# Sliding-window attention and a spectral mix on one core: q and k loaded as one block of long rows and transposed on 64x64 array tiles; the imaginary weight of mode 0 loaded again

## The chip, the cores and the metric

The kernel runs on one core of a Trainium2 chip. The time is the device time of one execution in microseconds (us). Of the kernel before, three runs are at hand: 453.2, 453.93 and 454.9 us, so the median is 453.93 us. The profiled execution took 453.2 us. Lower is better.

## The reference, cut to what matters

Two stages follow each other. The first is attention with 8 batches, 8 heads, 576 tokens and 64 values per head, in a causal window of 128 tokens with a slope per head. The second works on its output, `x` of 8 x 576 x 512:

```
scores = q @ k.T / 8 - slope[h] * |i - j|         where 0 <= i - j < 128, else -1e9
x      = softmax(scores) @ v                      heads side by side: 8 x 576 x 512
X      = rfft(x over the tokens)[:64 modes]
Y[m]   = (Xr + i Xi)[m] @ (w_r + i w_i)[m]        64 complex 512 x 512 weights
u      = x + irfft(Y)
out    = u + relu(u @ w_ch)
```

The inputs are float32. `q`, `k` and `v` are 9.4 MB each, the 128 matrices of `w_r` and `w_i` are 1 MB each. Mode 0 of a real signal has no imaginary part, and the inverse transform takes no notice of an imaginary part of `Y[0]`; so `w_i[0]` cannot change the output.

## The kernel before, in words

**Attention.** A unit is half a batch: four heads of one `b`, so there are 16 units. `load` (L198) has SyncE (SP) issue the transfers of a unit: one for q, one for k (L220) and three for v (L208, L213), into raw float32 buffers of which there are two each. `cast` (L226) lets VectorE (DVE) turn them into bfloat16, and issues the load of the unit two further on into the buffer that is thereby free. `transpose` (L243) has TensorE (PE) turn the cast q or k into `tp` in PSUM, and `evacuate` (L254) brings `tp` into `qkT` in SBUF, with the tokens in order; ScalarE (ACT) does this, except for q of the first two units, which are DVE's. `score` (L262) multiplies k by q on 64x64 array tiles, two heads on the two row halves of the array; for two of its four tiles it first adds a bias with the identity (L272). `exp` (ACT), `mask` (DVE, L306), `value` (PE, L332) and `norm` (DVE, L347 and L348) end the unit; `spectrum` (PE, L369) and `channels` (ACT, L387 and L388) take the batch's transform after every second unit, into the table `XC`.

The order of the work is written by hand: `STAGE` (L38) lists which step of which unit comes next, and each engine works its instructions off in that order. In one stage the transposition of k comes after `channels` and ahead of the next `score` with bias; that of q comes behind a `value` and ahead of a `score` without bias. `tp` has one buffer in PSUM, which `spectrum` uses too, so that the transposition of k waits for `channels` in each second unit.

How q and k lie: a head is 576 tokens of 256 bytes. In the kernel before, a partition holds 9 tokens each of two heads, which lie apart in memory: two rows of 2304 bytes. Partitions 0 to 63 hold heads 0 and 2, partitions 64 to 127 hold heads 1 and 3. The cast puts the two heads side by side, so that 9 transpositions of 128 x 128 (one for each token place `j`) make `tp`: head dimension of heads 0 and 1 in the upper half of the partitions and of heads 2 and 3 in the lower.

**The spectral mix.** `load_w` (L440) loads one weight of 1 MB. During attention GpSimd (POOL) issues 14 such loads that cast to bfloat16 on the way, held back by a small copy (`gate`, L520) that waits for a given `norm`; at the end of attention 6 more go into the raw buffers of q, k and v (L449). Then SP issues the rest as float32 (L453) into 6 and later 2 more buffers, and 8 more casting loads go into the first buffers to come free (`again`). For each weight PE makes four matmuls (L650) into `acc`; after each fourth mode the result is scaled (L543) and transposed (L547). From group 7 on, other work is put between the weights: the projection with `w_ch` of the first half of the modes (L623, L587, L609). Mode 0's imaginary weight, number 1 of 128, is in no list: `todo_w` (L438) leaves it out, and the loop passes over it (L645), so 127 weights are loaded. Once the last weight is multiplied, a last stage (L707 to L792) finishes and stores the output.

Of the kernel before, what the change touches and what calls it, by code (L numbers as in the profile page):

```python
# [10 lines left out]
FP32 = mybir.dt.float32  # L11
BF16 = mybir.dt.bfloat16
# [8 lines left out]
P = 128  # L21
D = 64
# [5 lines left out]
FULL = 4  # L28
TAIL = 64

TPP = 9

W = D + 2

# [72 lines left out]
class _Attention:  # L107
# [90 lines left out]
    def load(self, w, u):  # L198
        nc = self.nc
        if u >= len(self.units):  # L200
            return
        b, g = self.units[u]
        hs = slice(4 * g, 4 * g + 4)
        if w == "v":
            t = self.raw[w][:, u % 2]
            sv = self.v[b, hs]
            for pair in range(2):
                nc.sync.dma_start(  # L208
                    out=t[:, pair],
                    in_=sv[:, 2 * pair * P : 2 * (pair + 1) * P].rearrange(  # L210
                        "h (p j) d -> p h (j d)", j=2),
                )
            nc.sync.dma_start(  # L213
                out=t[64:96, 2],
                in_=sv[:, FULL * P :].rearrange("h (p j) d -> p h (j d)", j=2),
            )
        else:
            t = self.raw[w][:, u % 2]
            src = (self.q, self.k)["qk".index(w)][b, hs]
            nc.sync.dma_start(  # L220
                out=t.rearrange("p e j d -> p e (j d)"),
                in_=src.rearrange("(e h) (p j) d -> (h p) e (j d)", h=2, j=TPP),
            )
        self.loaded[w, u] = t

    def cast(self, u, w):  # L226

        nc = self.nc
        src = self.loaded.pop((w, u))
        if w == "v":  # L230
            src = src.rearrange("p s h (j d) -> p s h j d", j=2)
            for half in range(2):
                row = slice(64 * half, 64 * half + 64)
                nc.vector.tensor_copy(  # L234
                    self.vb[u % 2][row, :, :, :, W * half : W * half + D], src[row, :2])
            nc.vector.tensor_copy(self.vt[u % 2][64:96, :, :, :D], src[64:96, 2])
        else:
            dst = self.mid.tile([P, TPP, 2, D], BF16, tag=w, name=w)
            nc.vector.tensor_copy(dst.rearrange("p j e d -> p e j d"), src)  # L239
            self.casted[u, w] = dst  # L240
        self.load(w, u + 2)

    def transpose(self, u, w):  # L243
        nc = self.nc
        src = self.casted.pop((u, w))
        if (u, w) == (0, "k"):
            tp = self.ps.tile([P, TPP, P], BF16, tag="sc", bufs=2, name="tp")
        else:
            tp = self.ps.tile([P, TPP, P], BF16, tag="tp", name="tp")
        for j in range(TPP):  # L250
            nc.tensor.transpose(tp[:, j], src[:, j].rearrange("p e d -> p (e d)"), self.ident)  # L251
        self.open[w, u] = tp

    def evacuate(self, u, w):  # L254
        tp = self.open.pop((w, u))
        dst = self.qkT[u % 2][:, "qk".index(w), :, : self.S]
        (self.nc.vector.tensor_copy if u < 2 and w == "q" else self.nc.scalar.copy)(  # L257
            dst.rearrange("q h (p j) -> q h p j", j=TPP),
            tp.rearrange("q j (h p) -> q h p j", h=2),
# [138 lines left out]
def kernel(  # L398
# [10 lines left out]
    nc = tc.nc  # L409
    ctx.enter_context(tc.manual_schedule(engines=ALL | {SP}))  # L410
    B, H, S, _ = q.shape
    NM, DM, _ = moe_w_r.shape
    AHEAD = {0: 1, 1: 1, 2: 1, 4: 1, 5: 1, 7: 1, 8: 1, 10: 1, 11: 1, 12: 1, 13: 3, 14: 1}
    LATER = {14: 3, 15: 3}
    EARLY, NWA, NWB, AGAIN = 14, 6, 2, 8
# [12 lines left out]
    early = actx1.enter_context(  # L428
        tc.tile_pool(name="w1", bufs=EARLY, side="right", reuse_waits="tile")
    )  # L430
    rawpool = actx1.enter_context(tc.tile_pool(name="raw", bufs=1, side="right"))
    raw = {w: rawpool.tile([P, 2, 2, TPP, D], FP32, name=w + "r") for w in "qk"}
    raw["v"] = rawpool.tile([P, 2, 3, 4, 2 * D], FP32, name="vr")
    spare = [raw[w][:, i].rearrange("p e j d -> p (e j d)") for w in "qk" for i in range(2)]
    vflat = raw["v"].rearrange("p u s h d -> p (u s h d)")
    spare += [vflat[:, 2 * DM * i :] for i in range(3)]
    spare = [t[:, : 2 * DM].bitcast(BF16).rearrange("p (a e) -> p a e", a=4) for t in spare]
    wq, homes, todo_w, again = {}, {}, [0, *range(2, 2 * NM)], []  # L438

    def load_w(n, pool, bf16, chosen=None):  # L440


        for i in ([i for i in todo_w if i not in again][:n] if chosen is None else chosen):
            todo_w.remove(i)
            src = (moe_w_r, moe_w_i)[i % 2][i // 2].rearrange("(p a) e -> p a e", a=4)
            homes[i] = pool
            if bf16:
                t = spare.pop(0) if pool is None else pool.tile([P, 4, DM], BF16, tag="w", name="w")
                nc.gpsimd.dma_start(out=t, in_=src)  # L449
                wq[i] = [t[:, a] for a in range(4)]  # L450
            else:
                t = pool.tile([P, 4, DM], FP32, tag="w", name="w")
                nc.sync.dma_start(out=t, in_=src)  # L453
                wq[i] = [t[:, a].bitcast(BF16)[:, 1::2] for a in range(4)]

    with ExitStack() as actx:
# [43 lines left out]
        for h in (0, 2):  # L500
# [4 lines left out]
        side = {0: [(at.offset, 4), (at.offset, 6), (at.decay, 5), (at.offset, 5), (at.decay, 7),  # L505
                    (at.offset, 7), (at.decay, 4), (at.decay, 6)]}
        lags = [lag for _, _, lag in STAGE]
        for stage in range(min(lags), n + max(lags)):
            for name, arg, lag in STAGE:
                run(name, arg, stage - lag)  # L510
                if name in ("transpose", "exp") and side.get(stage):
                    for _ in range(1 + (name == "transpose")):
                        fn, h = side[stage].pop(0)
# [11 lines left out]
    with ExitStack() as mctx:  # L525
# [6 lines left out]
        again = [first + 4 + 2 * i for i in range(AGAIN)]  # L532
# [100 lines left out]
        def warm():  # L633
            wt = ps.tile([P, DM], FP32, tag="warm", bufs=1, name="warm")
            for _ in range(6):
                nc.tensor.matmul(wt, lhsT=ident, rhs=wch[:, 0], start=True, stop=True)  # L636

        quads, side, recycle = [], [], list(again)
        ZW = Z = XW = wch = w2 = None
        K1 = again[-1] + 1  # L640
        for g in range(NM // 4):
            acc = ps.tile([P, DM], FP32, tag="acc", bufs=2, name="acc")
            for i in range(8):
                m, ri = 4 * g + i // 2, i % 2
                if 2 * m + ri not in wq:  # L645
                    continue
                w = wq[2 * m + ri]
                for a in range(4):
                    c0 = (a * NC + (8 if ri == 0 else 0)) * NM + m
                    nc.tensor.matmul(  # L650
                        acc[32 * (i // 2) : 32 * (i // 2) + 32],
                        lhsT=XC[:, c0 : c0 + 31 * NM + 1 : NM],
                        rhs=w[a],
                        start=(ri == 0 and a == 0), stop=(ri == (m > 0) and a == 3),
                        tile_position=(0, 32 * (i // 2)),
                    )
                k = 8 * g + i
                if recycle:
                    load_w(1, early, True, [recycle.pop(0)])
                elif homes[k] not in (early, None):  # L660
                    load_w(1, homes[k], False)
                if k == K1 - 1:
                    actx1.close()
                    w2 = mctx.enter_context(
                        tc.tile_pool(name="w2", bufs=NWB, side="right", reuse_waits="tile")
                    )
                    load_w(NWB, w2, False)
                    right = mctx.enter_context(
                        tc.tile_pool(name="late", bufs=1, side="right", reuse_waits="tile")
                    )  # L670
                    wch = right.tile([P, 4, DM], BF16, name="wch")
                    nc.gpsimd.dma_start(out=wch, in_=moe_w_ch.rearrange("(a p) e -> p a e", p=P))
                    ZW = right.tile([P, B // 2, 2, DM], BF16, name="ZW")
                    Z = right.tile([P, B, DM], BF16, name="Z")
                    XW = right.tile([P, len(units), 2, DM], BF16, name="XW")

                if quads:
                    if next(quads[0], True):
                        quads.pop(0)
                elif side and k % 5:  # L680
                    side.pop(0)()
                elif 8 * g + i >= 2 * NM - 5:
                    if 8 * g + i < 2 * NM - 1:
                        warm()
            end = quad_end(acc, g)
            next(end)
            quads.append(end)
            if g == 7:
                side += [partial(early_spectra, bp) for bp in range(B // 2)]
                side += [partial(project, j, n) for j in range(len(units)) for n in range(2)]  # L690
# [132 lines left out]
```

## Time and profile before

| what | value |
|---|---|
| median of three runs | 453.93 us (453.2 to 454.9) |
| the profiled execution's own time | 453.2 us |
| its span, first to last instruction | 451.4 us |
| mean granted TensorE clock | 0.901 |
| PE busy | 351.5 us (78%), 3288 matmuls |
| DVE busy | 173.3 us (38%) |
| ACT busy | 154.6 us (34%) |
| read from HBM, written to it | 162.53 MB, 9.44 MB |
| attention | 0 to about 131 us |
| weights | PE's first matmul of a weight starts at 130.9 us, the last at 408.6 us |
| last stage | to 451.4 us |

How to read the lines of a profile: a group line names the line of the kernel, the engine, the operation, what it writes and reads, the shape and the count; behind the first bar stand the busy time in us and the mean of one in ns, behind the second the idle time of the engine just ahead of such instructions and what ended it. In a view by stretches of time, each engine's busy us stands with the number of instructions in brackets, then the granted clock, the mean busy share of the 16 DMA engines (over 1 where packets of one engine overlap) and the GB/s that they wrote. In the chain of waits and in the timeline the first number is the start in us, the second the length. A busy PE is not PE at its peak: matmuls are pipelined, and the next one starts long before the one ahead has ended.

### The profile page before, as it was taken

To read this page: it belongs to the slowest core of one execution; us is meant where nothing else is said; L and a number is where in the kernel's file an instruction comes from. 1 tells how busy PE (TensorE), PEld (TensorE's weight loads), DVE (VectorE), ACT (ScalarE), POOL (GpSimd) and SP (SyncE) were. 2 spreads that over 40 slices of the span, in tenths; PEclk is the share of its full clock that TensorE was granted. 3 is DMA by queue.
4 is the path that set the end of the run, shared out by engine and by line. 5 is a ranking of instruction groups with operands and counts; after the bars stand their busy time and mean duration, and the time that the engine had idled before them with its cause. 6 is when DMAs were issued, how large, how long until landed. Compare 5 with 4: busy or idle time off the path is not lost.

```text
span 451.4 us, 7816 instructions
## 1 busy us (share of the span) xinstructions
PE 351.5 (78%) x3288; PEld 186.2 (41%) x3288; DVE 173.3 (38%) x314; ACT 154.6 (34%) x191; POOL 54.6 (12%) x86
## 2 busy tenths in 40 slices
PE   4788999999876644456576679998989898987892
PEld 3466777777653212112121233443333343333230
DVE  7889899998732101001010241211111121103684
ACT  6868999999800000000000011221111121104671
POOL 8610101002411100000000000000000000000562
PEclk9999999999989655567666999999999899999998
DMA  8999999999999999999999999999999999990598
GB/s 285 325 333 310 310 305 309 316 284 249 212 303 316 315 318 315 340 395 422 420 422 418 424 421 418 420 422 419 422 421 420 417 422 421 419 399 8 212 345 282
DMA packets 51730, 157.26 MB, mean 348 GB/s; under 512 B 3696, under 2 KB 22640, under 8 KB 39024
## 3 DMA queue, kind: packets, MB, share of 16 engines
q1 hardware_dynamic: 47136, 141.57, 81.6%
q0 software_dynamic: 4560, 15.21, 17.0%
q8 instruction: 25, 0.41, 0.4%
q14 instruction: 9, 0.07, 0.0%
HBM read 162.53 MB, written 9.44 MB: 381 GB/s over the span
## 4 chain that ended last, share of the span: by engine, by line
DMA 54%; PE 24%; DVE 13%; ACT 4%; issue 3%; POOL 1%; ACTq 0%; SPq 0%; DVEq 0%; POOLq 0%
DMA w<-in_moe_w_i_dram 42%; PE acc L650 7%; DMA vr<-in_moe_w_i_dram 6%; DMA w<-in_moe_w_r_dram 4%; PE av L332 3%; PE my L623 2%; DVE vb L234 2%; DVE x L348 2%; DMA qr<-in_q_dram 2%; DVE att L306 2%; DVE q L239 2%; PE tp L251 2%; PE yy L754 1%; PE xt L369 1%; PE warm L636 1%
## 5 line engine op out<-in xcount | busy, mean ns | idle before, releaser
L650 PE MATMUL acc<-w,XC 128*32 128x512 bf16 x484 | 134.0, 465 | 59.8 <-DMA w<-in_moe_w_i_dram 38.6
L650 PEld LDWEIGHTS <-XC 128*32 128x32 bf16 x508 | 57.1, 141 | 126.6 <-issue 101.7
L295 ACT ACTIVATE att<-sc 128x1024 bf16<-128x1024 f32 x64 | 64.0, 1031 | 7.5 <-PE sc L285 7.5
L629 ACT CAST XW<-my 128x512 bf16<-128x512 f32 x36 | 21.1, 586 | 109.0 <-PE my L587 109.0
L735 POOL TENSOR_TENSOR r<-r,x 128x1024 f32<-128x1024 f32 x8 | 17.1, 2131 | 271.6 <-ACT r L733 271.5
L543 DVE TENSOR_SCALAR yq<-acc 128x512 bf16<-128x512 f32 x14 | 9.7, 690 | 100.9 <-PE acc L650 100.9
L571 ACT CAST ZW<-zw 128x512 bf16<-128x512 f32 x4 | 2.3, 586 | 133.5 <-PE zw L566 133.5
L611 DVE COPY xT<-tr 128x1024 bf16<-128x1024 bf16 x18 | 12.4, 692 | 90.6 <-PE tr L609 90.6
L332 PE MATMUL av<-vb,att 128*128 128x132 bf16 (+1 forms) x576 | 38.4, 217 | 5.4 <-DVE x L348 3.8
L332 PEld LDWEIGHTS <-att 128*128 128x128 bf16 x704 | 36.5, 98 | 11.0 <-DVE x L348 8.1
L623 PE MATMUL my<-wch,xT 128*64 128x512 bf16 x288 | 38.8, 392 | 0.8 <-DVE xT L611 0.8
L257 ACT COPY qkT<-tp 128x1152 bf16<-128x1152 bf16 x30 | 33.5, 1116 | 2.4 <-PE tp L251 1.8
L285 PE MATMUL sc<-qkT 64*64 64x256 bf16 (+2 forms) x640 | 25.5, 267 | 2.1 <-ACT qkT L257 1.2
L348 DVE TENSOR_TENSOR x<-av,rec 128x640 bf16<-128x640 f32 x32 | 26.4, 824 | 1.1
L768 DVE TENSOR_TENSOR o<-yy,r 128x1024 f32<-128x1024 f32 (+1 forms) x20 | 21.7, 1115 | 8.0 <-PE yy L754 4.2
L623 PEld LDWEIGHTS <-xT 128*64 128x64 bf16 x288 | 13.4, 110 | 23.3 <-issue 9.9
L285 PEld LDWEIGHTS <-qkT 64*64 64x64 bf16 x640 | 14.7, 110 | 19.1 <-issue 16.1
L234 DVE CAST vb<-vr 64x1024 bf16<-64x1024 f32 x32 | 22.2, 694 | 0.2
L272 PE MATMUL sc<-bias,ident 128*128 128x512 bf16 x64 | 20.3, 401 | 1.4 <-ACT att L295 1.4
L306 DVE TENSOR_TENSOR att<-att,mask 128x1024 bf16<-128x1024 bf16 x32 | 20.6, 683 | 0.0
L733 ACT ACTIVATE r<-mm 128x1024 f32<-128x1024 f32 (+1 forms) x19 | 17.7, 977 | 6.7 <-PE mm L587 6.5
L520 POOL COPY gate<-x 1x1 bf16<-1x1 bf16 x11 | 5.8, 525 | 84.9 <-DVE x L348 84.9
(105 smaller groups left out, 330.3 us busy)
## 6 DMA issues: line engine op xcount, KB each, us to landing
w<-in_moe_w_r_dram SPq DMA_DIRECT2D x53, 1024.0 KB, 18.7
w<-in_moe_w_i_dram SPq DMA_DIRECT2D x46, 1024.0 KB, 18.6
qr<-in_q_dram SPq DMA_DIRECT2D x16, 576.0 KB, 9.0
kr<-in_k_dram SPq DMA_DIRECT2D x16, 576.0 KB, 8.8
vr<-in_v_dram SPq DMA_DIRECT2D x32, 256.0 KB, 7.3
out_dram<-o SPq DMA_DIRECT2D x15, 512.0 KB, 3.9
w<-in_moe_w_i_dram POOLq DMA_DIRECT2D x14, 512.0 KB, 22.6
w<-in_moe_w_r_dram POOLq DMA_DIRECT2D x8, 512.0 KB, 8.2
```

What stands on the lines that cost most here:

```text
L234: nc.vector.tensor_copy(self.vb[u % 2][row, :, :, :, W * half : W * half + D], src[row, :2])
L257: (self.nc.vector.tensor_copy if u < 2 and w == "q" else self.nc.scalar.copy)(dst.rearrange("q h (p j) -> q h p j", j=TPP), tp.rearrange(" ...
L272: nc.tensor.matmul(sc[:, e], lhsT=self.ident, rhs=self.bias[:, hv].rearrange("p j n -> p (j n)"), start=True, stop=False, skip_group_check ...
L285: nc.tensor.matmul(sc[64 * half : 64 * half + 64, e, j * 256 + c0 : j * 256 + c0 + n], lhsT=qkT[row, 1, h, k0 + j : k0 + P : 2], rhs=qkT[r ...
L295: self.nc.scalar.activation(self.att[u % 2][:, kt * 8 * P : (kt + 1) * 8 * P], sc.rearrange("p e n -> p (e n)"), AF.Exp, scale=1.0 / math. ...
L306: nc.vector.tensor_tensor(out=rows, in0=rows, in1=self.table[:, heads], op=ALU.mult)
L332: nc.tensor.matmul(bank[:, qt * W : qt * W + rhs[j].shape[1]], lhsT=att[:, o : o + P], rhs=rhs[j], start=(n == 0 and j == 0), stop=(n == l ...
L348: nc.vector.tensor_tensor(out=self.x[:, b, :, cs].rearrange("p t (h d) -> p h t d", h=2), in0=tiles[:, :, :, :D], in1=rec.unsqueeze(-1).br ...
L623: nc.tensor.matmul(mm[ROWS[half]], lhsT=lhsT, rhs=wch[:, dt], start=(dt == 0), stop=False, skip_group_check=True,)
L629: nc.scalar.copy(XW[:, j, n], mm)
L650: nc.tensor.matmul(acc[32 * (i // 2) : 32 * (i // 2) + 32], lhsT=XC[:, c0 : c0 + 31 * NM + 1 : NM], rhs=w[a], start=(ri == 0 and a == 0), ...
L768: nc.vector.tensor_tensor(out=o[:, c], in0=yy[:, c], in1=r[:, c], op=ALU.add)
```

## The change

Two things change together.

First, q and k of a unit are loaded as one contiguous block: a partition holds 18 tokens of one head, one row of 4608 bytes, 32 partitions for each head. The cast then copies without rearranging. What was 9 transpositions of 128 x 128 becomes 36 of 64 x 64: for each of 18 token places two, one on the rows and columns 0 to 63 of the array and one on 64 to 127. `tp` has as many values as before, and `evacuate` reads it with 18 tokens in a row instead of 9 (L257; its text is the same, `TPP` is another).

Second, the imaginary weight of mode 0 is loaded and multiplied again: 128 weights in place of 127, and four matmuls more. The numbers of the 8 weights that are loaded a second way (`again`) move from the odd ones 25 to 39 to the even ones 24 to 38.

```diff
-TPP = 9
+TPP = 18
...
             nc.sync.dma_start(
-                out=t.rearrange("p e j d -> p e (j d)"),
-                in_=src.rearrange("(e h) (p j) d -> (h p) e (j d)", h=2, j=TPP),
+                out=t.rearrange("p j d -> p (j d)"),
+                in_=src.rearrange("h (p j) d -> (h p) (j d)", j=TPP),
             )
...
-            dst = self.mid.tile([P, TPP, 2, D], BF16, tag=w, name=w)
-            nc.vector.tensor_copy(dst.rearrange("p j e d -> p e j d"), src)
+            dst = self.mid.tile([P, TPP, D], BF16, tag=w, name=w)
+            nc.vector.tensor_copy(dst, src)
...
-            tp = self.ps.tile([P, TPP, P], BF16, tag="tp", name="tp")
+            tp = self.ps.tile([P, TPP, D], BF16, tag="tp", name="tp")
         for j in range(TPP):
-            nc.tensor.transpose(tp[:, j], src[:, j].rearrange("p e d -> p (e d)"), self.ident)
+            for e in range(2):
+                row = slice(64 * e, 64 * e + 64)
+                nc.tensor.transpose(tp[row, j], src[row, j], self.ident[row, row])
...
-    raw = {w: rawpool.tile([P, 2, 2, TPP, D], FP32, name=w + "r") for w in "qk"}
+    raw = {w: rawpool.tile([P, 2, TPP, D], FP32, name=w + "r") for w in "qk"}
...
-    wq, homes, todo_w, again = {}, {}, [0, *range(2, 2 * NM)], []
+    wq, homes, todo_w, again = {}, {}, list(range(2 * NM)), []
...
-                if 2 * m + ri not in wq:
-                    continue
                 w = wq[2 * m + ri]
...
-                        start=(ri == 0 and a == 0), stop=(ri == (m > 0) and a == 3),
+                        start=(ri == 0 and a == 0), stop=(ri == 1 and a == 3),
...
-                if recycle:
-                    load_w(1, early, True, [recycle.pop(0)])
+                if k < AGAIN:
+                    load_w(1, early, True, again[k : k + 1])
```

More of the change, by code (lines that the diff above doesn't have):

```diff
@@ L246, in transpose @@
         if (u, w) == (0, "k"):
-            tp = self.ps.tile([P, TPP, P], BF16, tag="sc", bufs=2, name="tp")
+            tp = self.ps.tile([P, TPP, D], BF16, tag="sc", bufs=2, name="tp")
         else:
-            tp = self.ps.tile([P, TPP, P], BF16, tag="tp", name="tp")
+            tp = self.ps.tile([P, TPP, D], BF16, tag="tp", name="tp")
         for j in range(TPP):
-            nc.tensor.transpose(tp[:, j], src[:, j].rearrange("p e d -> p (e d)"), self.ident)
+            for e in range(2):
+                row = slice(64 * e, 64 * e + 64)
+                nc.tensor.transpose(tp[row, j], src[row, j], self.ident[row, row])
         self.open[w, u] = tp
@@ L431 @@
     rawpool = actx1.enter_context(tc.tile_pool(name="raw", bufs=1, side="right"))
-    raw = {w: rawpool.tile([P, 2, 2, TPP, D], FP32, name=w + "r") for w in "qk"}
+    raw = {w: rawpool.tile([P, 2, TPP, D], FP32, name=w + "r") for w in "qk"}
     raw["v"] = rawpool.tile([P, 2, 3, 4, 2 * D], FP32, name="vr")
-    spare = [raw[w][:, i].rearrange("p e j d -> p (e j d)") for w in "qk" for i in range(2)]
+    spare = [raw[w][:, i].rearrange("p j d -> p (j d)") for w in "qk" for i in range(2)]
     vflat = raw["v"].rearrange("p u s h d -> p (u s h d)")
@@ L636, in warm @@
                 nc.tensor.matmul(wt, lhsT=ident, rhs=wch[:, 0], start=True, stop=True)
-        quads, side, recycle = [], [], list(again)
+        quads, side = [], []
         ZW = Z = XW = wch = w2 = None
```

## The prediction

> **What bounds the kernel now.** I read the page's busy shares, the chain of waits, the busy times by stretches of time, and the timeline of one stretch of attention.
>
> ```profile
> GB/s 285 325 333 310 310 305 309 316 284 249 212 303 316 315 318 315 340 395 422 420 422 418 424 421 418 420 422 419 422 421 420 417 422 421 419 399 8 212 345 282
> DMA 54%; PE 24%; DVE 13%; ACT 4%; issue 3%; POOL 1%; ACTq 0%; SPq 0%; DVEq 0%; POOLq 0%
> ```
>
> The chain has two regimes: up to 118 us it runs through DVE, PE and ACT, and after that through transfers of weights. By stretches (two units of attention each, then the stream of weights):
>
> ```profile
> 71.84:85.20 13.36, 12.62 (x236) 9.75 (x232) 12.69 (x25) 12.71 (x15) 1.10 (x2) 1.00 1.08 297
> 85.20:98.57 13.37, 12.62 (x236) 9.76 (x232) 12.38 (x23) 12.71 (x15) 2.09 (x4) 1.00 1.08 314
> ```
> ```profile
> 200.00:405.00 205.00, 168.60 (x921) 71.42 (x921) 29.95 (x62) 23.45 (x40) 0.00 (x0) 0.91 1.01 421
> ```
>
> From 200 to 405 us the 16 DMA engines are full (1.01) at 421 GB/s: the stream ends when its bytes are through. In attention PE (12.62 of 13.36 us), DVE and ACT (12.71) are all nearly full, so a little more on any of them can be seen. DMA is near full too (1.08), but the casts wait for a load only once in steady work: 1.7 us before the q cast at 26.91 us. Attention is paced by the engines, and its pace sets when the last casting loads start (109 to 118 us).
>
> ```profile
> 79.47 1.13 PE xt L369 x20
> 80.61 0.02 issue
> 80.63 0.59 ACT XC L387
> 81.22 0.29 ACT XC L388
> 81.51 0.04 issue
> 81.55 0.66 PE tp L251 x9
> 82.22 0.43 PE sc L272 x2
> ```
>
> This piece of the chain comes once in two units: the transposition of k waits for ACT, and the biased score for the transposition.
>
> **The extra weight: +2.5 us.** One load of 1.049 MB more (100 instead of 99 by SP). At 421 GB/s that is 1.049 / 0.421 = 2.49 us. Nothing hides it, as the share is 1.01 to 405 us; what follows (the tail to 451.4) moves with it. Below this only if the stream had holes, above it not at all. Its four matmuls (L650, mean 465 ns, overlapped: 4 in 1.06 us in the chain at full clock) come at about 131 us. There PE waits for transfers a little later (3.9 us for a load into `vr`, ending at 148.5 us), so they are hidden; without that cover they cost 1 to 1.6 us. The casting loads that POOL issues when PE lets buffers go (from 133 us) start up to 0.6 us later or not at all, behind loads in flight to 148 us: nothing. That they are even instead of odd weights changes no size.
>
> **The transpositions: 0.6 us for the changes of shape, nothing for themselves.** 32 groups (q and k of 16 units) go from 9 matmuls to 36, 864 more, with as many weight loads.
>
> ```profile
> L251 PE MATMUL tp<-ident,q 128*128 128x128 bf16 x144 | 12.0, 236 | 4.1 <-DVE q L239 4.1
> L251 PE MATMUL tp<-ident,k 128*128 128x128 bf16 x144 | 11.7, 231 | 1.5 <-ACT XC L388 1.1 <-DVE k L239 0.5
> L285 PE MATMUL sc<-qkT 64*64 64x64 bf16 x128 | 10.1, 193 | 0.0
> ```
>
> A mean of 236 ns is latency. In the trace's single starts the nine follow each other by 56 ns: 9 x 56 = 504 ns. The new shape is not in the trace as a transposition, but its size is: L285's 64-column matmuls on 64x64 tiles. In the score at 74.01 us a 64-column matmul starts at 74.131; the next weights for that tile are loaded from 74.132 on, and their matmul starts at 74.159, 28 ns after the one ahead. Its partner on the other row half runs 3 ns behind. So I take 28 ns for a pair: 18 x 28 = 504 ns, as now. The bounds: no lower than 27 ns (12 ns a group), no higher than one after the other, 36 x 28 = 1008 ns a group. I take the lower end because the nearest rows overlap. That two row halves may write one PSUM bank at once, as the new pairs do, shows here:
>
> ```profile
> 295.11 0.40 PE L587 MATMUL my<-ZW,FT 64*64 64x512 bf16 x2
> ```
>
> Two such matmuls of 512 columns, on opposite corners of the array and into one bank, took 0.40 us together; one alone has a mean of 401 ns.
>
> Two rules of the Trainium skill speak against this. "TensorEngine Tiling (Array Packing)", Gotcha 1, says that different row tiles cannot access one PSUM bank at the same time; if that stopped the pairs, a group would take twice as long. "TensorE: Matmul & The Clock Gate", LDWEIGHTS, lets a weight load take its columns / 1.2 ns, 53 ns for 64: a group would then be 18 x 53 = 0.96 us. The two rows above contradict both.
>
> The change of array shape: the steps between starts show 149 ns from a transposition to a score (64x64), where 56 would do, and 122 ns from a score to a transposition, where 28 would do. So each change costs some 94 ns. Their number stays the same; they move. That between score and transposition of k is hidden today in each second unit, under the wait for ACT (81.51 us above); afterwards it lies between transposition and L272, on the chain. Some 7 times x 0.094 = 0.66 us. That of q moves ahead of its group, so ACT's `evacuate` starts 0.09 us later; DVE's part of the chain covers this. If it did not, it costs another 0.7 us. I take 0.6.
>
> **Casts and evacuation: nothing.** L239's q cast takes 822 ns on average, median 750, the first one 691; L234, in runs of 64 like it, 694 for 1024 values. From 1024 to 1152 values that is the same rate, so rows of 64 cost nothing that a contiguous copy would save. Bounds: 691 ns each (two on the chain per two units, some 0.12 us x 7.5 = 0.9 us gained), or as now. L257 (1116 ns) moves as many values: nothing; up to 0.05 us x 15 = 0.8 us either way if runs of 18 differ from runs of 9.
>
> **The loads: -0.4 us.** Packets of 2304 bytes take 93 ns, of 8192 bytes 312 ns: a line through both gives 179 ns for 4608, where two now take 186. That is 0.06 us per load and 1.9 us of DMA in 32 loads, 4%. No engine waits for it in steady work, so it is hidden; the one stall (1.7 us at 25.2 to 26.9 us) shrinks by the 10 loads ahead of it, 0.6 us, of which I take 0.4. Bounds: 0 to 1.7 us gained; if every bit of DMA time counted, 1.9. SP issues each load in 0.4 us, before and after.
>
> **Sum.** 2.49 + 0.6 - 0.4 = +2.7 us. Against the profiled execution (span 451.4, own time 453.2) that is 455.9 us. This execution is the fastest of three; the median lies 0.7 us above, so I predict 453.93 + 2.7 = 456.6 us, 0.6% more. About 0.5% (2.3 us) is what can be told from no change here, so this is slower by little.
>
> **Rivals.**
>
> 1. *The pairs run one after the other.* For it: the two halves of a pair write the same bank, and no transposition on tiles is in this trace. Against it: L285 and L587. Price: 504 ns more per group, 4 groups in two units, 2.0 us; PE has 13.36 - 12.62 = 0.74 us left, so 1.3 to 2.0 us x 8 = 10 to 16 us with the weight on top: 466 to 473 us. Half way (40 ns for a pair): 0.86 us in two units, 457 to 464 us.
>
> 2. *Faster: DVE casts the contiguous block at another rate.* For it: DVE carries casts on the chain (0.76 and 0.67 us in two units), and a copy of 64x512 from bfloat16 (L356) takes 286 ns, half as much per value. Against it: the source is float32 as before, and L234's rate. Place: two casts on the chain per two units. It decides from about 0.2 us saved per cast (a cast under 0.55 us): 0.4 x 8 = 3.2 us cancels the rest. At the most ACT becomes the bound: 13.37 - 12.71 = 0.66 us x 8 = 5.3 us, so 453.9 + 3.1 - 5.3 = 451.7 us.
>
> 3. *The loads gain what the weight costs, or nearly so.* The stall at 26.9 us goes entirely (-1.7) and the moved changes of shape hide: 453.9 + 2.5 - 1.7 = 454.7 us. For it: DMA is full all through attention. Against it: PE was busy until 27.33 us at that stall, and only DVE gains.
>
> **How the numbers follow.** Forecast 0.65 (455.5 to 457.8; three quarters of it above 456.2, the bound of 0.5%), rival 1 0.16, rival 2 0.09, rival 3 0.10. Slower: 0.48 + 0.16 = 0.64; same: 0.17 + 0.10 = 0.27; faster 0.09. The range takes in the forecast with its bounds, rival 3, the small half of rival 2 (from 452.6) and the half-way case of rival 1 (to 463).
>
> **What would show it.** After: L650 with 512 weight loads in place of 508, and 100 loads by SP in place of 99; the stretch from 200 to 405 us at 421 GB/s as now, and its end later. The 64x64 transpositions in groups of 36 of about 0.67 us from first start to last end, as now 0.66; 1 us or more would be rival 1. Two units of attention in 13.4 to 13.5 us, and the first weight matmul at 130.5 to 132 us. The casts at 750 ns; under 550 would be rival 2. I am wrong if attention shifts by over 1 us either way, or if the stream of weights is shorter than 2.5 us more.

## The result, and the profile after

The changed kernel takes **467.5 us** (median of 4 runs, 465.72 to 470.07); the kernel before, on the same chip, 454.41 us. The ratio is 1.0295, 95% interval [1.024, 1.0349]: 13 us slower, where 2.7 were forecast. The direction was right, and the time lies above the range given (to 463 us). The profiled execution took 465.72 us, with a span of 463.9 against 451.4: +12.5 us. It splits like this:

| stage | before | after | more |
|---|---|---|---|
| start to the first matmul of a weight | 130.9 us | 141.5 us | 10.6 |
| first to last matmul of a weight | 277.7 us | 279.9 us | 2.1 |
| last stage | 42.8 us | 42.5 us | -0.3 |

So the loss lies in attention. These lines of the page after answer to those shown of before (GB/s by slices of 11.6 us, the chain by engine, the instruction loads, and ACT's evacuation):

```profile
span 463.9 us, 9554 instructions
...
GB/s 289 311 315 323 276 259 312 303 240 243 171 239 314 316 315 316 322 374 427 420 420 421 422 420 420 422 417 421 423 420 418 422 419 421 420 417 38 181 341 293
...
q8 instruction: 32, 0.52, 0.5%
...
DMA 52%; PE 30%; DVE 6%; ACT 5%; issue 4%; ACTq 0%; POOL 0%; DVEq 0%; POOLq 0%
...
L259 ACT COPY qkT<-tp 128x1152 bf16<-128x1152 bf16 x30 | 33.5, 1117 | 11.6 <-PE tp L253 11.1
```

Three things stand out. PE's share of the chain rose from 24 to 30%, and DVE's fell from 13 to 6%: in attention the chain now runs through PE's transpositions and ACT's evacuation (L259, no slower itself at 1117 ns), and ACT stands idle 11.1 us for them, against 1.8 before. There are 9554 instructions in place of 7816. And queue q8, which brings instructions, carried 32 packets in place of 25.

The two clean pairs of units, and the stream of weights, by stretches:

```profile
62.20:76.10 13.90, 13.09 (x356) 10.23 (x350) 12.52 (x23) 12.60 (x14) 1.04 (x2) 1.00 0.99 297
68.68:82.52 13.84, 13.21 (x360) 10.23 (x354) 12.47 (x23) 12.61 (x15) 2.15 (x4) 1.00 1.01 301
200.00:405.00 205.00, 166.89 (x897) 69.42 (x896) 30.77 (x65) 22.87 (x39) 0.00 (x0) 0.88 1.02 419
```

Two units take 13.84 us where nothing disturbs them, 0.47 more than the 13.37 of before; for 7.5 such pairs that is 3.5 us of the 10.6. DVE (12.47) and ACT (12.61) have as much work as before. The stream is as full as it was (1.02, 419 GB/s).

The other 7 us are not in the pace. From a unit's second `norm` to the next one's, before alternates between 6.26 and 7.11 us in steady work; after has 7.72, 11.17, 7.37, 6.45, 7.38, 6.46, 9.28, 7.03, 7.6 in a row: some units take far longer. The timeline of PE in one of them (last column: the idle time ahead, and what ended it):

```profile
82.16 0.69 PE L253 MATMUL tp<-ident,q 64*64 64x64 bf16 x32
82.66 0.30 PE L287 MATMUL sc<-qkT 64*64 64x256 bf16 x2
82.68 0.23 PE L253 MATMUL tp<-ident,q 64*64 64x64 bf16 x4
82.75 0.27 PE L287 MATMUL sc<-qkT 64*64 64x256 bf16 x1
83.84 0.62 PE L287 MATMUL sc<-qkT 64*64 64x256 bf16 x13 [0.82 <-issue]
```

PE stops in the middle of a score, three of whose matmuls it has already begun, and goes on 1.09 us after the start of the last one. "issue" says that nothing in the profile held it: no semaphore, no transfer of data. The waits of PE from 20 to 125 us with that end (total us, times, longest):

```profile
PE tp L253 <- issue: 2.3, 3, 1.0
PE av L334 <- issue: 0.8, 1, 0.8
PE sc L287 <- issue: 0.8, 1, 0.8
PE xt L371 <- issue: 0.2, 1, 0.2
```

4.1 us, on four different lines; before has none. A wait that belongs to no line suggests that PE had no instruction to work on. The records of q8 fit: its packets have 16,384 bytes, and PE's 8312 matmuls and weight loads are 32.5 blocks of 256, where q8 carried 32 packets (6576 are 25.7 blocks, with 25 packets, before). So a packet is taken as 256 of PE's instructions, of 64 bytes each. Each of the six standstills ends as long after the landing of such a packet; the last column counts the matmuls and weight loads that PE had begun by then:

| kernel | packet landed, us | PE goes on, us | between | PE's instructions begun |
|---|---|---|---|---|
| after | 37.35 | 38.71 | 1.36 | 1215 |
| after | 43.51 | 44.90 | 1.39 | 1471 |
| after | 82.45 | 83.84 | 1.39 | 3263 |
| after | 89.42 | 90.86 | 1.44 | 3519 |
| after | 94.81 | 96.23 | 1.42 | 3775 |
| after | 106.39 | 107.80 | 1.41 | 4287 |

The last column shows where PE stops: divided by 256, every one of these numbers leaves 191, and the quotient (4, 5, 12, 13, 14, 16) is the number of packets that have landed by then. The same holds for all 16 standstills in the traces of three kernels below (7 in `tiles_only`, 7 in `split_before`, 2 in `k_tiles`). So PE stands still only at the border of two packets, until the next one has landed.

By the stretches, PE takes 356 matmuls and 350 weight loads in 13.90 us, 51 instructions per us; before it was 236 and 232 in 13.36 us, 35 per us. So a packet of 256 lasts 5.0 us in place of 7.3. Whether the number of instructions makes the packets late, or something else in the change, these times do not say.

### The profile page after: what moved, and what is told of

The parts are those of the page before. It is cut to its first block, busy times and chain, and to the rows that moved or that the text cites. A ratio compares the mean times of both kernels' runs of the same rounds, so it can differ in the third digit from the quotient of the medians.

```text
span 463.9 us, 9554 instructions
## 1 busy us (share of the span) xinstructions
PE 366.8 (79%) x4156; PEld 193.5 (42%) x4156; DVE 173.6 (37%) x314; ACT 154.5 (33%) x191; POOL 54.2 (12%) x86
## 4 chain that ended last, share of the span: by engine, by line
DMA 52%; PE 30%; DVE 6%; ACT 5%; issue 4%; ACTq 0%; POOL 0%; DVEq 0%; POOLq 0%
DMA w<-in_moe_w_i_dram 32%; DMA w<-in_moe_w_r_dram 12%; PE acc L650 7%; DMA vr<-in_moe_w_i_dram 6%; PE av L334 4%; PE tp L253 4%; ACT att L297 2%; PE sc L274 2%; PE my L625 2%; DMA qr<-in_q_dram 2%; PE sc L287 2%; PE yy L754 1%; PE warm L638 1%; PE mm L714 1%; DVE q L239 1%
## 5 line engine op out<-in xcount | busy, mean ns | idle before, releaser
L650 PE MATMUL acc<-w,XC 128*32 128x512 bf16 x488 | 146.3, 456 | 55.1 <-DMA w<-in_moe_w_r_dram 33.4
L650 PEld LDWEIGHTS <-XC 128*32 128x32 bf16 x512 | 59.5, 140 | 129.2 <-issue 98.9
L334 PE MATMUL av<-vb,att 128*128 128x132 bf16 (+1 forms) x576 | 38.6, 217 | 5.4 <-DVE x L350 3.1
L334 PEld LDWEIGHTS <-att 128*128 128x128 bf16 x704 | 36.7, 98 | 11.2 <-DVE x L350 6.5
L259 ACT COPY qkT<-tp 128x1152 bf16<-128x1152 bf16 x30 | 33.5, 1117 | 11.6 <-PE tp L253 11.1
L287 PE MATMUL sc<-qkT 64*64 64x256 bf16 (+2 forms) x640 | 27.3, 270 | 2.8 <-ACT qkT L259 1.2
L287 PEld LDWEIGHTS <-qkT 64*64 64x64 bf16 x640 | 16.1, 111 | 19.0 <-issue 17.5
L274 PE MATMUL sc<-bias,ident 128*128 128x512 bf16 x64 | 21.3, 418 | 2.2 <-ACT att L297 2.2
L253 PE MATMUL tp<-ident,q 64*64 64x64 bf16 x576 | 13.7, 202 | 5.8 <-DVE q L239 3.9
```

What stands on the lines that cost most here:

```text
L253: nc.tensor.transpose(tp[row, j], src[row, j], self.ident[row, row])
L274: nc.tensor.matmul(sc[:, e], lhsT=self.ident, rhs=self.bias[:, hv].rearrange("p j n -> p (j n)"), start=True, stop=False, skip_group_check ...
L287: nc.tensor.matmul(sc[64 * half : 64 * half + 64, e, j * 256 + c0 : j * 256 + c0 + n], lhsT=qkT[row, 1, h, k0 + j : k0 + P : 2], rhs=qkT[r ...
L334: nc.tensor.matmul(bank[:, qt * W : qt * W + rhs[j].shape[1]], lhsT=att[:, o : o + P], rhs=rhs[j], start=(n == 0 and j == 0), stop=(n == l ...
L650: nc.tensor.matmul(acc[32 * (i // 2) : 32 * (i // 2) + 32], lhsT=XC[:, c0 : c0 + 31 * NM + 1 : NM], rhs=w[a], start=(ri == 0 and a == 0), ...
```

## The experiments

The theory to test, S in the expectations: the 1728 additional instructions of PE (864 matmuls, as many weight loads) are more than its supply brings while the DMA engines are full. The rivals, P and L among them, put the cost into the transpositions (the array's time, or their place on the path) or into the loads.

### The weight alone, and the tiles alone

`weight_only` is the kernel before with mode 0's imaginary weight:

```diff
-    wq, homes, todo_w, again = {}, {}, [0, *range(2, 2 * NM)], []
+    wq, homes, todo_w, again = {}, {}, list(range(2 * NM)), []
...
-                if 2 * m + ri not in wq:
-                    continue
```

> The kernel before with only the imaginary weight of mode 0 loaded and multiplied again. Theory S (PE runs dry of instructions in attention, because 36 small transpositions with their weight loads are 72 instructions where there were 18), theory P (the pairs' own pace and the changes of array shape cost it) and theory L (the loads in long rows and the contiguous cast cost it) all say the same here: the weight alone costs one transfer of 1.05 MB, 2.1 to 2.5 us, so about 456.5 us, and attention ends where it did (first weight matmul at about 131 us).

457.73 us against 454.47: 1.006 [1.0036, 1.0083], which is +2.7 us by the ratio. Its first weight matmul starts at 131.88 us, and the stream is as it was:

```profile
200.00:405.00 205.00, 166.91 (x912) 70.38 (x909) 29.98 (x62) 23.45 (x40) 0.00 (x0) 0.90 1.01 421
```

`tiles_only` is the changed kernel with the same edit turned round:

```diff
-    wq, homes, todo_w, again = {}, {}, list(range(2 * NM)), []
+    wq, homes, todo_w, again = {}, {}, [0, *range(2, 2 * NM)], []
...
+                if 2 * m + ri not in wq:
+                    continue
```

> The changed kernel without the extra weight: long rows, contiguous cast and 64x64 transpositions, mode 0's imaginary weight left out as before. All three theories: attention 10 to 11 us longer, the stream of weights as before, so about 465 us. If the parts help or hurt one another, this and weight_only will not add up to the whole 13 us.

466.21 us, 1.0255 [1.0201, 1.031], which is +11.7 us; the first weight matmul starts at 141.79 us. The standstills are there as well, 5.6 us from 20 to 125 us:

```profile
PE tp L253 <- issue: 3.0, 4, 1.1
PE xt L371 <- issue: 1.5, 1, 1.5
PE sc L287 <- issue: 0.8, 1, 0.8
PE av L334 <- issue: 0.3, 1, 0.3
```

The two gains in the ratios add up to 1.0315, and both changes at once make 1.0295: the parts neither help nor hurt one another measurably, and what was not foreseen lies in this half of the change.

### Half of each pair

The changed kernel without the weight, in which from the third unit on only the upper transposition of each pair is made, and the upper half evacuated.

```diff
-            for e in range(2):
+            for e in range(2 if u < 2 else 1):
                 row = slice(64 * e, 64 * e + 64)
...
+        if u >= 2:
+            dst, tp = dst[:64], tp[:64]
```

> As tiles_only, but from the third unit on only the upper transposition of each pair is made (18 matmuls of 64x64 per group, one every 28 ns) and only the upper half is evacuated, so half of the transposed q and k is that of an older unit: it leaves work out. A group is as long as the nine big ones were (504 ns), the changes of array shape and the loads are as in tiles_only, and the instructions per group are 36 instead of 72. Theory S: most of the loss is gone, 455 to 458 us, and PE's waits without a releaser of about 0.8 us are gone. Theory P, if the changes of shape carry the loss: 460 us or more. Theory L: 465 us.

457.1 us, 1.0053 [1.0035, 1.0071]. PE has 7296 instructions in place of the 8304 of `tiles_only`, no wait of PE from 20 to 125 us ends with "issue", and the clean pair of units takes 13.71 us. In the chain:

```profile
89.36 0.55 PE tp L253 x18
89.91 0.54 PE sc L276 x2
```

With half the transpositions 9 of the 11.7 us are gone, although a group still is 18 steps on the array. The 2.4 us that are left are about what the slower pace makes, 0.34 x 7.5 = 2.6 us. That alone decides for neither theory: it takes instructions away, but also the second half of each pair.

### As many instructions, no tiles

So the other way round: the kernel before, with the matmuls of `value`, of the bias and of `spectrum` cut into narrower ones. The array passes as many columns, the transpositions and the loads stay, and PE has 8176 instructions, 1600 more.

```diff
-                nc.tensor.matmul(
-                    sc[:, e], lhsT=self.ident, rhs=self.bias[:, hv].rearrange("p j n -> p (j n)"),
...
+                for c in range(0, 512, 128):
+                    nc.tensor.matmul(
+                        sc[:, e, c : c + 128], lhsT=self.ident, rhs=bias[:, c : c + 128],
...
+                    for c in range(0, rhs[j].shape[1], W):
...
+                for r in range(2):
```

> The kernel before with its big transpositions and its loads, but matmuls of value, of the bias and of the spectrum cut into parts of fewer columns (132 into 2 x 66, 512 into 4 x 128, 128 into 2 x 64), so that PE gets 1600 more instructions in attention for the same columns, nearly as many as the change brings (1728), and no array shape changes more than before. Theory S: PE runs dry as in the changed kernel, 4 to 8 us more, 458 to 462 us, with waits of about 0.8 us that no semaphore ends. Theories P and L: 454 to 455.5 us, as only a few ns per cut are added.

466.17 us, 1.0249 [1.021, 1.0287]: as slow as `tiles_only`, without one of its tiles. The first weight matmul starts at 142.9 us. PE's waits from 20 to 125 us, and the timeline at one of them:

```profile
PE sc L287 <- issue: 1.9, 3, 1.2
PE av L335 <- issue: 1.7, 1, 1.7
PE xt L374 <- issue: 1.6, 1, 1.6
PE sc L274 <- issue: 0.5, 1, 0.5
PE tp L251 <- issue: 0.3, 1, 0.3
```
```profile
102.28 0.30 PE L287 MATMUL sc<-qkT 64*64 64x256 bf16 x2
103.79 0.41 PE L287 MATMUL sc<-qkT 64*64 64x192 bf16 x10 [1.22 <-issue]
```

6.0 us on five lines, two of them (the scores of L287, the transpositions of L251) not touched. The three longest end 1.35 to 1.56 us after a packet of 16,384 bytes landed (102.25 us for the one shown). This is theory S: the number of instructions brings the standstills, whatever the instructions are. But the loss is larger than the 4 to 8 us expected, and the standstills are not all of it: the clean pair of units takes 13.79 us here, with extra instructions of another kind, and in the profiled execution the granted clock was 0.5 for 6.8 us from 20.5 us on and for 3.4 us from 58.1 us on.

### The loads and the cast alone

The kernel before with q and k loaded as one block in rows of 4608 bytes and cast contiguously, but nine transpositions of 128 x 128.

```diff
-                out=t.rearrange("p e j d -> p e (j d)"),
-                in_=src.rearrange("(e h) (p j) d -> (h p) e (j d)", h=2, j=TPP),
+                out=t.rearrange("p j d -> p (j d)"),
+                in_=src.rearrange("h (p j) d -> (h p) (j d)", j=TPP),
...
+            nc.tensor.transpose(
+                tp[:, j], src[:, 2 * j : 2 * j + 2].rearrange("p e d -> p (e d)"), self.ident)
```

> Loads in rows of 4608 bytes and the contiguous cast of the change, without the extra weight, but transposed by nine 128x128 matmuls that take two token places at once: the instructions of the kernel before, on a layout in which scores meet values in the wrong order, so the output is not the reference's. Theory L (long rows and the contiguous cast carry a part of the loss): over 457 us. Theories S and P, by which all of it lies in the small transpositions: 453 to 455 us, two units of attention in 13.37 us as before, at the best 1 us less where a q cast waited for its load.

454.87 us against 454.69: 0.9991 [0.9969, 1.0013]. The long rows and the contiguous cast are worth nothing that can be measured; no trace shows the pace of its units.

### q alone, k alone

Each is the kernel before with one of the two loaded, cast and transposed the new way; PE has 7440 instructions in both.

```diff
-        for j in range(TPP):
-            nc.tensor.transpose(tp[:, j], src[:, j].rearrange("p e d -> p (e d)"), self.ident)
+        for j in range(TPQ if w == "q" else TPP):
+            if w == "k":
...
+                continue
+            for e in range(2):
+                row = slice(64 * e, 64 * e + 64)
+                nc.tensor.transpose(tp[row, j], src[row, j], self.ident[row, row])
```

> Only q goes the new way (long rows, contiguous cast, 36 matmuls of 64x64); k is loaded and transposed as before; no extra weight. PE has 864 instructions more than before instead of 1728. Theory S: half the instructions, so nearly no standstill of PE, as in half_pairs; what stays is the later evacuation of q on ACT, 2 to 3 us: 455.5 to 457.5 us. If the loss goes with the number of tile transpositions (theory P), half of it stays: 460 us.

457.17 us, 1.0053 [1.0027, 1.0078]; the clean pair of units takes 13.55 us.

> The mirror of q_tiles: only k goes the new way, q is loaded and transposed as before; no extra weight; as many instructions as q_tiles. If what is left of the loss at half the instructions comes from q's evacuation on ACT, which the change of array shape ahead of q's group makes later, little is left here: 0.3 to 1.5 us over before, two units of attention in 13.4 to 13.5 us instead of q_tiles' 13.55. If it comes from the number of instructions or of pairs, it is q_tiles again: 2 to 3 us over before, 13.55 us.

456.72 us, 1.0047 [1.0029, 1.0065]; 13.57 us. After `q_tiles` I thought that q carries what the standstills leave over, by its later evacuation. That **fell**: k costs as much. The chain at k's transposition, first in `k_tiles`, then in `q_tiles`, where k is as before:

```profile
83.09 0.76 PE tp L269 x36
83.85 0.54 PE sc L290 x2
84.39 0.35 PE sc L303 x8
```
```profile
83.25 0.66 PE tp L265 x9
83.91 0.43 PE sc L290 x2
84.34 0.35 PE sc L303 x8
```

The group takes 0.10 us more and the biased score behind it 0.11: together 0.21, the 0.20 us by which two units are longer. For q the same sum comes by way of ACT, which gets `tp` later. Both together make 13.37 + 0.18 + 0.20 = 13.75, near the 13.84 of after. Each alone costs 2 to 3 us, and both 11.7: the sum does not rise evenly with the instructions. At 7440, standstills are few (one of 0.8 us in `q_tiles`, 0.5 and 0.3 in `k_tiles`); at 8304 they are 5.6 us.

### Fewer bytes beside the instructions

If instructions come late because the DMA engines are full, taking other bytes away must bring them in time. `tiles_light` is `tiles_only` with v loaded for the first two units only; `before_light` is before with the same cut.

```diff
-        if w == "v":
+        if w == "v" and u >= 2:
+            t = self.raw[w][:, u % 2]
+        elif w == "v":
```

> tiles_only, but v is loaded for the first two units alone and used again by the others (a third of q, k and v is not read, the output is not the reference's), so that the DMA engines have gaps in attention. If PE runs dry because its instructions queue behind data on the DMA engines, the waits of 0.8 us and more shrink or go: 2 to 5 us above before_light. If an instruction load is slow by itself, they stay: 10 to 12 us above before_light.

> The kernel before with v loaded for the first two units alone, the control of tiles_light. Attention of the kernel before waits for no load but one of 1.7 us at the start, so 451 to 454.5 us.

`tiles_light`: 458.6 us, 1.0078 [1.0049, 1.0106]; `before_light`: 453.02, 0.9952 [0.9924, 0.998]. So the tiles cost 5.6 us with light loads (3.2 in the profiled spans, 454.5 and 451.3), where they cost 11.7 with all; 2 to 5 were expected. First `tiles_only`, then `tiles_light`, by the same stretch, and the waits that end with "issue" from 20 to 125 us, in `tiles_light` and in its control `before_light`:

```profile
58.00:112.00 54.00, 48.45 (x1245) 37.18 (x1245) 45.63 (x81) 45.65 (x51) 6.20 (x12) 1.00 0.98 276
```
```profile
58.00:112.00 54.00, 48.42 (x1318) 39.48 (x1330) 48.99 (x88) 48.61 (x55) 5.50 (x11) 1.00 0.74 192
```
```profile
PE sc L289 <- issue: 0.4, 1, 0.4
```
```profile
PE sc L287 <- issue: 0.7, 2, 0.4
```

The control has waits of the same length at the same line (the score) and no tiles, and none of these three lies at the border of two packets; so they are no standstills of this kind. With the DMA engines 0.74 busy in place of 0.98, the same instructions run without standstills, 73 matmuls more in the same 54 us. In the profiled execution the 3.2 us that are left match the slower clean pace (3.5). That execution is the fastest of ten, though, and the median costs 2.4 us more; whether standstills return in the others is not shown.

As far as the records go, what is late is a packet's turn on the engines. From the start of a packet's first instruction on PE to the start of the next packet on the DMA engines, the traces have 2.9 us in before, 2.8 in `tiles_only` and 2.0 in `tiles_light` (medians from 20 to 125 us, counted by PE's weight loads). The packet itself takes 1.0 us in all three, and PE goes on some 1.4 us after its landing. By this estimate a packet needs 2.8 + 1.0 + 1.4 = 5.2 us in `tiles_only`, where the one ahead lasts 5.0; 4.4 in `tiles_light`; and 5.3 in before, where it has 7.3. What part of the 2.8 us is queueing no record separates.

### A weight that is loaded later

To see whether attention's end can be had cheaper, before with the first casting load moved from stage 0 to stage 3.

```diff
-    AHEAD = {0: 1, 1: 1, 2: 1, 4: 1, 5: 1, 7: 1, 8: 1, 10: 1, 11: 1, 12: 1, 13: 3, 14: 1}
+    AHEAD = {1: 1, 2: 1, 3: 1, 4: 1, 5: 1, 7: 1, 8: 1, 10: 1, 11: 1, 12: 1, 13: 3, 14: 1}
```

> The kernel before with the first casting load of a weight (stage 0, at 17.8 us) moved to stage 3, so that the third unit's q, which lands 1.7 us late at 26.9 us, has not that 1 MB ahead of it on the DMA engines. A try at a version that beats both: 0.5 to 1.7 us less than before if the shorter start carries through to the stream of weights; the same if attention's pace takes it up.

454.19 us against 454.45, 0.9996 [0.9979, 1.0013]: no gain. No kernel that does all of the work is measurably faster than the one before.

## Why the prediction was wrong, point by point

**The failed step** is "The transpositions: 0.6 us for the changes of shape, nothing for themselves". It counted the 864 matmuls more, "with as many weight loads", and then priced only their time on the array. Their price as instructions to be brought to PE was left out, and no rival had it. In its place `tiles_only` shows +11.7 us: 5.6 us of standstills at the borders of packets, and 0.47 us more for each two units of clean work. The sign of being wrong that the prediction had set itself, attention shifting by over 1 us, came with 10.6.

- *The time on the array was nearly right.* In single starts the pairs follow each other by 31.6 ns (75.817, 75.848, 75.880, 75.912, 75.943 us), the partner 3 ns behind; 28 was taken. The two halves do write one bank at once. A group of k in the chain takes 0.76 us, with 0.67 forecast and 0.66 before; one after the other would be 1 us or more. (The bound of 27 ns for a pair makes a group 18 ns shorter, not 12; nothing rests on it.) After:

```profile
72.95 0.76 PE tp L253 x36
73.71 0.54 PE sc L274 x2
```

- *Rival 1 named the right time by the wrong mechanism.* 467.5 us lies in its 466 to 473, but the pairs overlap, and `split_before` loses as much without any pair. A number that fits does not confirm a cause.
- *The changes of shape: right in kind, too small.* The steps between starts show what the prediction said (lines of the changed kernel): from a transposition to the biased score (L253 to L274) it went from 56 to 125 ns, from a `value` to a transposition (L334 to L253) from 33 to 124, from a transposition to a score without bias (L253 to L287) from 149 to 29. So 0.09 us moved onto the path. But the steps of 31.6 in place of 28 ns come on top, and q's later evacuation, said to be covered by DVE's part of the chain, is not: `q_tiles` shows 0.18 us for two units. In place of 0.6 us the clean pace costs 0.47 x 7.5 = 3.5 us.
- *The standstills: not in the sum.* 4.1 us of "issue" stand in the trace from 20 to 125 us. The remaining 10.6 - 3.5 - 4.1 = 3.0 us of attention are not attributed: each standstill also makes ACT and DVE late, and the granted clock was 0.5 for 3.4 us from 49.4 us on, in this execution. In `tiles_only`, whose clock was full in attention, the same sum leaves 10.9 - 3.5 - 5.6 = 1.8 us.
- *The extra weight: right.* 2.49 us forecast; 2.1 in the trace, 2.7 from `weight_only`.
- *Casts and evacuation: right.* The trace has the q cast at 821 ns and the evacuation at 1117, against 822 and 1116:

```profile
L239 DVE CAST q<-qr 128x1152 bf16<-128x1152 f32 x16 | 13.1, 821 | 2.3 <-DMA qr<-in_q_dram 2.3
```

- *The loads: nothing, where 0.4 us were expected.* A packet of 4608 bytes takes 180 ns, as forecast (179); q lands in 8.4 us in place of 9.0, k in 7.4 in place of 8.8; but the wait at the start is 2.3 us in place of 1.7. `block_big` leaves no room for rivals 2 and 3.

What could have been read beforehand: the page of before has queue q8 with 25 packets (0.41 MB) on DMA engines that the prediction itself called near full (1.08), and the counts in brackets give PE's 35 instructions per us; the edit raised that by nearly half.

## What to carry to other kernels

Count an edit's instructions as well as its busy time: many small ones in a stage where the DMA engines are full can leave an engine without instructions, and the profile shows that as "issue" on arbitrary lines, ending shortly after a packet of the instruction queue lands and a multiple of 256 instructions apart. To test it, put as many instructions into the old kernel by splitting other work, and take bytes away from the new one; the two together tell supply from execution. And an operation moved out of a hidden place costs on the path what it always cost.

## What the runs showed of the hardware

- **Instructions come in packets of 16,384 bytes on the DMA engines, and PE can run out of them.** The instruction queue from 20 to 125 us, before and then after (packets, MB, share of the engines' time):

```profile
q8 instruction: 13, 0.21, 0.8%
```
```profile
q8 instruction: 18, 0.29, 1.2%
```

  1% of the DMA time, and yet it holds up the kernel: PE stands still for 4.1 us after the change, 6.0 in `split_before`, not at all with the engines at 0.74 (`tiles_light`). The Trainium skill describes this supply ("Runtime: NRT & Kernel Launch", Instruction fetch mechanics): blocks of 16 KiB, 256 instructions, fetched over DMA while the ones ahead are worked off. The size agrees with the packets, and with the distance between standstills, always a multiple of 256 instructions. The page also holds that the fetch stays hidden behind the issue of instructions; here that does not hold at 51 instructions per us beside full DMA engines.
- **Pairs of 64-column transpositions on opposite 64x64 tiles run every 31.6 ns**, weight loads included, into one bank (the starts at 75.817 to 75.943 us above).
- **A change of array shape costs 91 to 94 ns on PE**, in both kernels and in either direction (steps of 149 in place of 56 ns and 122 in place of 28 before, 125 in place of 31.6 and 124 in place of 33 after); an edit that keeps their number can still move them to where they count.
